# Output stores of a fused convolution and SiLU block: issued on Pool's queue instead of SyncE's

## The chip, the cores and the metric

The kernel runs on one core of a Trainium2 chip. The metric is the device time of one execution in microseconds, the median of several runs. Engines are named as in the profile: PE (TensorE), DVE (VectorE), ACT (ScalarE), POOL (GpSimd) and SP (SyncE, which computes nothing and here only issues DMAs).

## What is computed

Shapes: x is 8 x 4096 x 192, weight 8 x 7, w_in 192 x 2048, w_out 2048 x 192, all float32 as the kernel uses them.

```python
w = softmax(weight, axis=-1)                        # one 7-tap filter for each of 8 heads
x_pad = np.concatenate([zeros(B, 6, D), x], axis=1) # causal padding
out = np.einsum('hk,bskhg->bshg', w, windows(x_pad))
x = out.reshape(B * S, D)                           # 32768 x 192
h = x @ w_in                                        # "up" products
g = h * (1.0 / (1.0 + np.exp(-h)))                  # SiLU
return g @ w_out                                    # "down" products
```

## The kernel before, in words

The 32768 tokens are cut into 32 blocks of 1024, numbered 0 to 31. A block is two halves of 512 tokens, which lie in the two halves of the partitions. It goes through these stages:

- `load` (L181) brings x of a block into the tile `nat`, in three parts (tokens ld.0 to ld.2) of four DMAs.
- `turn_in` (L465, token i) transposes on DVE into `xt`. `halo_in` (token ha) fills the six columns ahead of it: Pool copies or clears the head of the first half (L486, L480), SP moves the second half's (L487). `tail_of` (L475) keeps the last columns for the next block.
- `conv` (token v) makes the seven taps: the first on ACT (L496), six on DVE (L499), back into `nat`.
- `spread` (L516, token sp) copies the result to both halves of the partitions, into `dup`, by DMA on SP. `win` (L533, L536, token w) makes sums and differences of it.
- `product` (L625, token P) and `plain` (L642, token L) are the up products on PE. The kernel uses a scheme with fewer products in place of ordinary ones; `sums_h` (L668, L674, L686) puts the pieces together on DVE and ACT and takes the SiLU into the tiles `g`.
- `sum_g` (L709, token t) subtracts pieces of `g` on DVE into tiles `t`: t.j0 and t.j1 go into one tile, t.j2 and t.j3 into another, for j from 0 to 3. `out_slot` (L741, token D) makes the down products on PE; D`i`.`je` stands for output piece i from chunk j, half e. `merge` (L804, L819) puts the output pieces together in `cmb`.
- `turn_out` (L829, token o) transposes `cmb` on DVE into the tile `osb`, in four parts o.0 to o.3. `store_out` (L838, token st) writes each part to `out_dram` with three DMAs of 64 KB, in rows of 128 bytes: 12 for a block.

`t` and `osb` share a pool of three buffers, and an osb is one buffer until all of its four parts are stored:

```python
tpool = ctx.enter_context(tc.tile_pool(name="tp", bufs=3))
    t[i // 2] = tpool.tile([P, 2, 2 * TB], F32, tag="t", name="t")
    osbs[b] = tpool.tile([P, 4, TB // SQ, SQ], F32, tag="t", name="osb")
```

The order of the work is written out by hand. `PLAN` is a string of tokens that is run once for each block; a token with "-" works on the block before, "=" on the one two before, "+" on the next. `pin` keeps the order of instructions on each engine and queue as the tokens give it; the head copy and clearing in `halo_in` on Pool are not pinned. In PLAN the tokens around the stores come in this order (others left out):

```
P5.0 ... | -D0.00 -t.01 | -D1.00 =o.2 | -D2.01 -t.03 | =st.2 | ... -t.02 | -D4.00 -t.10 | -t.11 | ... -t.12
... -t.13 | ... -o.1 | ... -st.1 | ... +ld.0 | ... sp.1 | ... +ha.0 | ... -st.0 | -st.3 ... t.00
```

So st.2 is the last of a block's stores, two turns after its up products, and t.10 of the next block comes soon after it. Semaphores are set by the framework from the tiles that instructions read and write.

The last block, 31, is stored by `finish` (L944) on SP's and ACT's queues. Blocks 0 and 1 are stored in a start-up order, `START`. In steady turns Pool runs one short instruction (L486 or L480).

Of the kernel before, what the change touches and what calls it, by code (L numbers as in the profile page):

```python
# [17 lines left out]
def kernel(  # L18
# [24 lines left out]
    nc = tc.nc  # L43
# [111 lines left out]
    def pin(ins):  # L155
        return tc.keep_in_program_order(ins)
# [677 lines left out]
    def store_out(b, i):  # L834
        for q in range((HD if b else P) // SQ):
            n, c = (i % 2, HD * (i // 2) + SQ * q) if b else (q // 2, R * i + SQ * (q % 2))
            pin(
                nc.sync.dma_start(  # L838
                    out=out_v[2 * b + n][:, :, c : c + SQ],
                    in_=osbs[b][SQ * q : SQ * q + SQ, i, :, :],  # L840
                )
            )
# [15 lines left out]
    def step(b, token):  # L858
# [19 lines left out]
        elif name[0] in "uXabS":  # L878
            sums_h(b, name, *digits)
        elif name == "t":  # L880
            sum_g(b, *digits)
        elif name[0] == "D":
            i, (j, e) = int(name[1]), digits
            for half in range(2) if i == 3 and b == NB - 1 else (None,):
                out_slot(b, j, i, e, half)
        elif name[0] in "Mzyx":
            merge(b, name, *digits)
        elif name == "o":
            turn_out(b, *digits)
        elif name == "st":  # L890
            store_out(b, *digits)
        elif name == "dp":
            next(downs)
        elif name == "cp":
            copy_plain(b, *digits)
        elif name == "go":
            pool.tensor_copy(warm, nats[1][:, digits[0], 0, 0:1])
            for g in (2, 3):
                for e in range(2):
                    combine(g, e)  # L900
        elif name == "ld":
            if b + 1 < NB:
                load(b + 1, digits)
        elif b + 1 < NB:
            {"i": turn_in, "ha": halo_in, "v": conv, "sp": spread, "w": win}[name](
                b + 1, *digits[: 1 + (name == "v")]
            )
# [203 lines left out]
```

## Time and profile before

| | |
|---|---|
| median of 3 runs | 2349.09 us (2348.8 to 2349.61) |
| the profiled execution | 2349.19 us, its span 2347.5 us |
| one turn of PLAN, from the timeline | 72.15 us |
| share of the span: PE, DVE, ACT, POOL | 100%, 89%, 51%, 4% |
| store `out_dram<-osb`, 64 KB, on SP | 376 issues, 2.0 us from issue to landing (median) |
| one store issue on SP (L838) | 0.50 us (median) |
| `dup<-nat`, 128 KB, on SP | 345 issues, 2.3 us to landing |
| `nat<-in_x_dram`, 64 KB, on SP | 382 issues, 2.4 us to landing |
| SP waiting at L838 for the transpose L829 | 1250.1 us in all, 66 times |

The span runs from the first to the last instruction; the execution's own time is 1.7 us longer. A row of the timeline has the start in us, the length in us, the engine (with "q" where only its queue works, as in issuing a DMA), the line, the operation, what it writes and reads, the shapes, how many instructions are merged in the row, and in brackets the idle time before it with what ended it. A row of a table by stretches has the stretch and its length, the busy us and instructions of PE, PEld (weight loads), DVE, ACT and POOL, then the granted clock of PE, the share of the DMA engines and GB/s. Matmuls overlap each other, so a row of one matmul is longer than the time from one start to the next.

### The profile page before, as it was taken

The numbers are of one execution on the slowest core, as the hardware profiler recorded it, in microseconds if no ns is written. First come the engines' busy times: TensorE is split into PE (matmuls) and PEld (weight loads), VectorE is DVE, ScalarE is ACT, GpSimd is POOL, SyncE is SP. The second block draws the span as 40 slices with busy tenths as digits, with TensorE's granted clock in tenths as the row PEclk, the third lists the DMA queues.
The fourth block names the chain that finished last, engine by engine and source line by source line (L and its number), as shares of the span: only waits on it lengthen the run. The fifth ranks groups of instructions, "written<-read, shape, count | busy, mean of one in ns | idle before, by whom it ended". The sixth has DMA issues, their size and how long they took to land.

```text
span 2347.5 us, 43988 instructions
## 1 busy us (share of the span) xinstructions
PE 2340.3 (100%) x17630; PEld 1061.0 (45%) x17630; DVE 2099.6 (89%) x2877; ACT 1187.3 (51%) x2275; POOL 96.8 (4%) x168
## 2 busy tenths in 40 slices
PE   9999999999999999999999999999999999999998
PEld 4344444444444444434444444444444444444445
DVE  8899989899899998998998999989999989899876
ACT  4345644456544466444564445654446644456443
POOL 4920000000000000000000000000000000000000
PEclk9999999999999999999999999999999999999999
DMA  7232212222121221222221222212222212222111
GB/s 158 52 66 48 47 27 47 38 53 53 29 41 36 53 53 31 39 43 46 53 49 31 42 38 53 53 29 42 36 53 53 38 33 45 43 53 44 20 24 25
DMA packets 451245, 106.56 MB, mean 45 GB/s; under 512 B 423584, under 2 KB 428704, under 8 KB 451040
## 3 DMA queue, kind: packets, MB, share of 16 engines
q1 hardware_dynamic: 447392, 101.78, 23.7%
q8 instruction: 138, 2.26, 0.4%
q0 software_dynamic: 448, 1.58, 0.3%
q10 hardware_dynamic: 3200, 0.39, 0.1%
q14 instruction: 67, 0.55, 0.1%
HBM read 31.46 MB, written 25.17 MB: 24 GB/s over the span
## 4 chain that ended last, share of the span: by engine, by line
PE 99%; DVE 0%; ACT 0%; issue 0%; ACTq 0%
PE ps L741 47%; PE ps L625 42%; PE ps L642 5%; PE ps L762 2%; PE ps L571 2%; PE ps L1010 1%; PE ps L423 0%; DVE t L709 0%; ACT g L686 0%; DVE cmb L163 0%; ACT u L163 0%; DVE osb L163 0%; DVE osb L829 0%; DVE g L668 0%; PE ps L449 0%
## 5 line engine op out<-in xcount | busy, mean ns | idle before, releaser
L625 PE MATMUL ps<-win,wr 64*128 64x512 f32 x1550 | 720.3, 597 | 0.0
L741 PE MATMUL ps<-g,wo 128*32 128x512 f32 x2976 | 702.4, 593 | 0.0
L625 PE MATMUL ps<-win,ws 64*128 64x512 f32 x1550 | 631.3, 595 | 0.0
L741 PE MATMUL ps<-t,wo 128*32 128x512 f32 (+2 forms) x4528 | 545.7, 446 | 0.0
L674 ACT COPY u<-ps 128x512 f32<-128x512 f32 x775 | 446.8, 586 | 173.6 <-PE ps L625 161.4
L741 PE MATMUL ps<-t,wx 128*32 128x512 f32 x2976 | 495.5, 592 | 0.1
L625 PE MATMUL ps<-dup,wr 64*128 64x512 f32 x868 | 425.4, 593 | 0.0
L499 DVE SCALAR_TENSOR_TENSOR nat<-xt,taps,nat 128x512 f32<-128x512 f32 x564 | 411.3, 753 | 3.8 <-ACT nat L496 3.6
L686 ACT ACTIVATE g<-g 128x512 f32<-128x512 f32 x465 | 286.1, 633 | 231.5 <-DVE g L668 231.5
L804 ACT COPY yx<-ps 32x512 f32<-32x512 f32 x150 | 86.9, 579 | 574.0 <-PE ps L741 572.3
L709 DVE TENSOR_TENSOR t<-g 128x1024 f32<-128x1024 f32 x248 | 300.6, 1219 | 51.1 <-PE ps L741 43.4
L625 PEld LDWEIGHTS ps<-win,wr 64*128 64x128 f32 x1550 | 275.6, 186 | 150.4 <-issue 67.8
L668 DVE TENSOR_TENSOR g<-u,ps 128x512 f32<-128x512 f32 x465 | 311.2, 680 | 28.8 <-PE ps L625 14.6
L625 PE MATMUL ps<-dup,ws 64*128 64x512 f32 x682 | 324.2, 599 | 0.0
L709 DVE TENSOR_TENSOR t<-g,t 128x1024 f32<-128x1024 f32 x248 | 301.8, 1217 | 12.2 <-PE ps L741 9.4
L741 PEld LDWEIGHTS ps<-t,wo 128*32 128x32 f32 x4528 | 186.7, 110 | 274.1 <-issue 247.6
L625 PEld LDWEIGHTS ps<-win,ws 64*128 64x128 f32 x1550 | 254.7, 186 | 110.5 <-issue 40.8
L686 ACT ACTIVATE g<-ps 128x512 f32<-128x512 f32 x465 | 266.8, 597 | 41.1 <-PE ps L625 38.4
L668 DVE TENSOR_TENSOR ps<-u,ps 128x512 f32<-128x512 f32 x310 | 214.7, 692 | 43.7 <-ACT g L686 19.0
L741 PE MATMUL ps<-g,wx 128*32 128x512 f32 x1488 | 250.5, 592 | 0.0
L741 PEld LDWEIGHTS ps<-g,wo 128*32 128x32 f32 x2976 | 170.2, 110 | 120.9 <-issue 118.9
L741 PEld LDWEIGHTS ps<-t,wx 128*32 128x32 f32 x2976 | 120.5, 110 | 217.5 <-issue 202.3
(90 smaller groups left out, 1764.5 us busy)
## 6 DMA issues: line engine op xcount, KB each, us to landing
dup<-nat SPq DMA_DIRECT2D x345, 128.0 KB, 2.3
nat<-in_x_dram SPq DMA_DIRECT2D x382, 64.0 KB, 2.4
out_dram<-osb SPq DMA_DIRECT2D x376, 64.0 KB, 2.0
raw<-in_moe_w_out_dram SPq DMA_DIRECT2D x8, 384.0 KB, 3.6
raw<-in_moe_w_in_dram SPq DMA_DIRECT2D x12, 192.0 KB, 4.7
ws<-wr POOLq DMA_DIRECT2D x8, 192.0 KB, 5.0
raw<-in_moe_w_in_dram SPq DMA_DIRECT2D x6, 128.0 KB, 3.1
xt<-xt SPq DMA_DIRECT2D x31, 4.5 KB, 1.9
```

Source lines behind the costliest of these rows:

```text
L499: nc.vector.scalar_tensor_tensor(out=dst, in0=src, scalar=tap, in1=dst, op0=ALU.mult, op1=ALU.add)
L571: nc.tensor.matmul(hs[a, n, e], rows(wr[j], e)[:, a, k, :], rows(d, e)[:, n, k, :], start=k == 0, stop=k == NK - 1,)
L625: nc.tensor.matmul(to[:, cols], raw(g, *LEFT[e][r], e), rhs[:, cols], start=first, stop=True, skip_group_check=True,)
L642: nc.tensor.matmul(banks[PLAIN_BANKS[n and 1 + e]][:, cols], rows(wr[j] if own == e else ws[j], e)[:, a, k, :], rows(dups[b], e)[:, SLOT[e ...
L668: pin(nc.vector.tensor_tensor(out_, u, v, op=op))
L674: pin(nc.scalar.copy(us[b, g, o][:, cols], t1[:, cols]))
L686: pin(nc.scalar.activation(h, src, AF.Silu))
L709: pin(nc.vector.tensor_tensor(t[i // 2][:, i % 2, :], u, v, op=ALU.subtract))
L741: nc.tensor.matmul(accs[b][at][SQ * q : SQ * q + SQ, to], lhs[:, e, SQ * k : SQ * k + SQ], rhs[:, e, ts(q, TB // 4) if i == 5 else to], st ...
L762: nc.tensor.matmul(banks[DOWN_BANKS[k]][R * n : R * n + R, :], wo[j][:, a, e, R * k : R * k + R], gs[b, j, a][:, n, e, :], start=j == 0 an ...
L804: pin(nc.scalar.copy(to, acc[3 * (name[0] == "x") + k][n:P, :]))
L1010: nc.tensor.matmul(by_pe[k][n], rows(diag, n)[:, k, i, :], rows(xts[0], n)[:, k, i : i + TB], start=i == 0, stop=i == K - 1,)
```

## The change

From block 2 on, `store_out` issues its DMAs from Pool (GpSimd) instead of SP. Where the stores stand in the order of tokens, what they move and the tiles are as before. `finish` is as before, too.

```diff
@@ -835,7 +835,7 @@
         for q in range((HD if b else P) // SQ):
             n, c = (i % 2, HD * (i // 2) + SQ * q) if b else (q // 2, R * i + SQ * (q % 2))
             pin(
-                nc.sync.dma_start(
+                (nc.gpsimd if b > 1 else nc.sync).dma_start(
                     out=out_v[2 * b + n][:, :, c : c + SQ],
                     in_=osbs[b][SQ * q : SQ * q + SQ, i, :, :],
                 )
```

## The prediction

> **What bounds the kernel now.** I read the page's first part, then the busy time of each engine in four block-long stretches, then the waits, then the timeline of one block.
>
> ```profile
> PE 2340.3 (100%) x17630; PEld 1061.0 (45%) x17630; DVE 2099.6 (89%) x2877; ACT 1187.3 (51%) x2275; POOL 96.8 (4%) x168
> ...
> PE 99%; DVE 0%; ACT 0%; issue 0%; ACTq 0%
> ```
> ```profile
> 1150.31:1222.45 72.14, 72.14 (x553) 32.69 (x552) 65.28 (x90) 37.15 (x72) 0.19 (x1) 1.00 0.24 43
> 1222.45:1294.60 72.15, 72.15 (x554) 32.72 (x553) 65.29 (x90) 37.16 (x72) 0.19 (x1) 1.00 0.24 43
> 1727.40:1799.55 72.15, 72.15 (x553) 32.66 (x552) 65.30 (x90) 37.15 (x72) 0.19 (x1) 1.00 0.24 43
> 1799.55:1871.70 72.15, 72.15 (x553) 32.80 (x552) 65.30 (x90) 37.17 (x72) 0.19 (x1) 1.00 0.24 43
> ```
>
> TensorE is busy all through, and every block takes 72.15 us. VectorE works 65.3 of those, Pool 0.2, so a change reaches the end only if it holds up PE. The queue view shows no PE wait that ends in a DMA. One transfer does hold up VectorE:
>
> ```profile
> DVE t L709 <- DMA out_dram<-osb: 5.7, 6, 1.3
> ```
>
> The subtraction L709 waits six times for a store (5.7 us in all, 1.3 at most). The timeline says which one. An ordinary block:
>
> ```profile
> 1223.77 0.70 DVE L829 STREAM_TRANSPOSE osb<-cmb 96x512 f32<-96x512 f32 x1
> ...
> 1224.49 1.41 SPq L838 DMA_DIRECT2D out_dram<-osb  x3
> 1226.00 4.33 SPq L516 DMA_DIRECT2D dup<-nat  x7
> ...
> 1227.89 1.21 DVE L709 TENSOR_TENSOR t<-g 128x1024 f32<-128x1024 f32 x1
> 1229.14 1.23 DVE L709 TENSOR_TENSOR t<-g,t 128x1024 f32<-128x1024 f32 x1
> 1230.28 1.22 DVE L709 TENSOR_TENSOR t<-g 128x1024 f32<-128x1024 f32 x1
> ```
>
> The last transpose of a block (token o.2) ends at 1224.47, its three stores (st.2) follow, and t.10 starts at 1227.89. The pool of `t` tiles has three buffers, two of them hold t.00 to t.03, and the third is the osb that these stores read: t.10 needs all three landed. Stores land 2.0 us after issue, so at about 1227.4: half a microsecond in hand.
>
> A block where SP was slow to issue the same three stores:
>
> ```profile
> 1801.63 2.89 SPq L838 DMA_DIRECT2D out_dram<-osb  x3
> ...
> 1806.41 1.23 DVE L709 TENSOR_TENSOR t<-g 128x1024 f32<-128x1024 f32 x1 [1.31 <-DMA out_dram<-osb]
> ...
> 1810.61 1.22 DVE L709 TENSOR_TENSOR t<-g,t 128x1024 f32<-128x1024 f32 x1
> ...
> 1812.07 1.15 PE L741 MATMUL ps<-t,wo 128*32 128x512 f32 x12
> ```
>
> The issues took 1.48 us more, t.10 started 1.31 us late, and the stretch from 1799.55 still took 72.15. So 1.31 us of lateness is free. But hardly more: t.13 (the row at 1810.61) ends at 1811.83, and the product that reads it, D3.11, starts at 1812.07 after a weight load of 0.13. About 0.1 us is left, so **PE's tolerance is about 1.4 us**.
>
> **What the Trainium skill says.** "DMA: Bandwidth & Descriptors", section "SWDGE vs HWDGE vs iDMA": a DMA from Pool has its descriptors computed by software on Pool's cores, one from SP by hardware. The same page, "Latency and other measured facts", gives the first byte as about 1 us against 0.6. The trace agrees in direction: the same kind of halo load (L198, 384 elements of 4 bytes) landed 3.0 and 3.1 us after issue from Pool, 2.6 from SP. The section "Issuing engines are not separate DMA queues" says that all issuers share the same 16 DMA engines, and a second issuer saves only issue time; nothing in this trace speaks against it. "SBUF — State Buffer", section "Who interferes with whom", has VectorE instructions with two SBUF inputs contend with Pool instructions that read SBUF. Here L499 takes 0.75 us in steady blocks and 0.94 (median) between 85 and 125 us, while Pool combines weights; whether Pool's descriptor writing does the same no row shows.
>
> **The change, part by part.** Stores of blocks 2 to 30 move: 29 blocks of 12, 348 issues.
>
> *Removed from SP.* 12 issues of 0.47 us, 5.6 us a block, and the waits for osb (1250.1 us over the run, 66 times). Behind them on SP stand nat loads, dup copies and the halo copy. They go earlier, but nobody waits for them now (VectorE waited 0.7 us once for a nat load; PE never for dup), so this is worth 0. One side effect: the seven dup copies behind st.2 can go when the last product on the old dup is done, about 1222.5 instead of 1226.0, and so share the DMA engines with st.2. DMA share is near 0.9 while they run.
>
> *Added to Pool.* 12 issues at 0.7 to 0.9 us (L198: 0.87 and 0.72) make some 10 us in a 72 us block. Pool has room. In its queue stands one other job, the head copy L486 (0.19 us, at 1199.22). The order of tokens puts it after st.1 (osb ready at 1196.4) and before st.0 (ready at 1208.2), and even after st.0 or st.3 it would be done by about 1214, where the halo transfer it goes with lands (issued by SP at 1212.61, 1.9 us). Worth 0; if that cover went, the scaled copy L496 at 1217.15 would still leave 3 us.
>
> *st.1, st.0, st.3.* Later landings by a microsecond or two are hidden: the tile is not given back before st.2, at least 11 us on.
>
> *st.2, the part that counts.* On SP the third store starts 0.91 us after the first and lands 2.0 later: 2.9 from release. On Pool, with L198's prices: the third starts 0.87 + 0.72 = 1.59 after release and lands 3.1 later: 4.7. Shift: 1.8. The slow-issue block turned a shift of 1.48 into a lateness of 1.31, so 0.17 comes off: 1.6. Added: 512 elements instead of 384 (a 64-element Pool DMA, L347, took 0.523; (0.717 - 0.523)/320 is 0.6 ns an element, 0.08 for each of two issues), 0.15; and the dup traffic, 0.15 by my estimate, for which no row stands. Lateness of t.10: **about 1.9 us**. Above the tolerance: 0.5 us. PE is full, so what it loses there it doesn't make good. The wait falls on t.10 of blocks 4 to 31, 28 of them: 28 x 0.5 = 14 us.
>
> Behind t.10 on VectorE stand t.11 to t.13, a conv tap, and t.20. These pass the lateness to D2.11 (t.11 ends at 1230.37, its weight load is at 1232.57: 2.2 us of slack) and D3.11 (1.4). After that it melts: t.20, t.23 and t.30 wait 0.43, 0.20 and 1.19 us for PE in an ordinary block.
>
> *Bounds.* Below: a Pool issue of 0.52 (second of an L347 pair) and a landing of 2.4 (SP's 2.0 plus the 0.4 by which L198 differed) give 1.04 + 2.4 = 3.4, lateness 0.4, loss 0. Above: L347 landed 4.4 to 6.7 us after issue (192 KB, beside the heavy loads of the start); 1.6 + 5.0 = 6.6 is a lateness of 3.5, a loss of 2.1 a block, 59 us. Contention that slows VectorE is inside this upper bound. No gain is excluded by PE alone: its loads also wait for VectorE and ScalarE in the up products, some tenths of a microsecond a block.
>
> **Sum.** The profiled execution took 2349.19 (span 2347.5 and 1.7 around it), 0.1 over the median 2349.09. 2349.2 + 14 = 2363.
>
> **The rivals.**
>
> *The stores land in time* (0.30): no change, so not slower. It is decided at t.10: if the third store lands within about 1.6 us of its present time (1.4 of lateness and 0.17), D3.11 finds t.13 ready, and the time is 2349. For it: 1.31 us was absorbed, and the lower bound gives 0.4. The buffer could also be given out otherwise, t.10 taking the one that D4.00 frees at about 1228.7; then it is late by 0.9 whatever the stores do. Against it: both L198 landings.
>
> *Pool's descriptor writing and VectorE get in each other's way* (0.15): at 1224.5 to 1228 VectorE runs t.03, a tap and t.02, all with two SBUF inputs. If each Pool issue waits for one (1.2 us), the third store starts 2.4 after release, not 1.6, and if VectorE loses as much, lateness is near 3.3: loss 1.9 x 28 = 53, time 2402. For it: L499 under Pool load. Against: L347's issues took 0.52 beside a busy VectorE.
>
> *SP's freed queue helps* (0.05): dups and loads in hand early. PE loses some tenths a block to late VectorE in the up products; regaining 0.3 in 28 blocks gives 2341. Against: those waits are for arithmetic, not transfers.
>
> *That the edit does nothing* is excluded unless the stores stayed on SP's queue; the issue rows would tell.
>
> **How the numbers follow.** Late store, small loss: 0.50, 2363. A measurement here can tell about 0.2%, 4.7 us, from no change; a loss of 0.17 us a block is that bound. Part of the likeliest case lies below it, roughly balanced by the in-time case lying just above. Slower 0.50 + 0.15 = 0.65; same 0.30; faster 0.05. Range 2347 to 2398: from no change to a lateness of 3.1 (28 x 1.7 = 48 us), leaving out most of the faster case and the top of the contention case.
>
> **What the changed profile would show.** Right: st.2's issues on Pool at 0.7 to 0.95 us; landing near 3; nearly every t.10 waiting 1.5 to 2.5 us for out_dram<-osb; a loads-wait of PE for t at D3.11; the down products (in the timeline 35.7 us from the first start, 1222.45, to the last) longer by half a microsecond, the up products as now. Wrong: t.10's wait under 1.4 and blocks of 72.15; or long Pool issues with L499 or L709 slower than 0.75 and 1.22; or a block that grows outside the down products, which would put the cause elsewhere.

## The result, and the profile after

The kernel with the stores on Pool's queue takes **2355.44 us** (median of 9 runs, 2354.01 to 2356.58) against 2349.09 (9 runs, 2348.8 to 2349.8): 1.0026 times the time before, 95% interval 1.0017 to 1.0035. That is slower by 6.35 us, on the side that was forecast, and less than half of the 14 us forecast. The profiled execution took 2355.44 us with a span of 2353.5, so 6.0 us more span than before.

The page of the profile after:

```profile
span 2353.5 us, 44146 instructions
...
PE 2346.0 (100%) x17630; PEld 1102.3 (47%) x17630; DVE 2100.2 (89%) x2877; ACT 1187.4 (50%) x2275; POOL 321.1 (14%) x516
...
q0 software_dynamic: 11584, 24.41, 6.4%
q8 instruction: 138, 2.26, 0.4%
...
PE 98%; DVE 1%; ACT 0%; DMA 0%; issue 0%; SPq 0%; POOL 0%; DVEq 0%; ACTq 0%
...
L838 POOL DMA_DIRECT2D out_dram<-osb x348 | 223.9, 649 | 1880.2 <-DVE osb L829 1873.3
...
L709 DVE TENSOR_TENSOR t<-g 128x1024 f32<-128x1024 f32 x248 | 302.1, 1218 | 59.1 <-DMA out_dram<-osb 37.9
```

The edit did what it says: 348 stores issue on Pool (516 instructions there instead of 168) and travel on a queue of their own, q0. VectorE's sum is as before (2100.2 against 2099.6). PE's busy time grew by 5.7 us with the same 17630 matmuls: matmuls overlap, so a PE that is held up still counts as busy nearly all the time, and the loss must be looked for elsewhere. The last two rows say where: L709 now has `out_dram<-osb` as the main thing that ends its waits. The list of waits, with total, times and longest:

```profile
DVE t L709 <- DMA out_dram<-osb: 37.9, 26, 3.2
```

Before it was 5.7 us in 6 times, 1.3 at most. So t.10 does meet the stores in nearly every turn, as forecast. The idle time of VectorE before t.10 is called its lateness here; the longest is 3.2 us. The loss is not even over the turns. Two turns in a row (stretch, length, then PE, PEld, DVE, ACT, POOL, clock, DMA share, GB/s); I call the first one turn 3 and count on from it:

```profile
357.00:429.14 72.14, 72.14 (x553) 32.74 (x553) 65.28 (x90) 37.15 (x72) 7.92 (x13) 1.00 0.23 43
429.14:502.92 73.78, 73.30 (x553) 37.68 (x552) 65.29 (x90) 37.13 (x72) 7.83 (x13) 1.00 0.23 42
```

The first takes what a turn took before, the second 1.64 us more. The timeline of turn 3, which lost nothing:

```profile
354.52 4.32 SPq L516 DMA_DIRECT2D dup<-nat  x7
...
358.31 0.70 DVE L829 STREAM_TRANSPOSE osb<-cmb 96x512 f32<-96x512 f32 x1
...
359.31 1.93 POOL L838 DMA_DIRECT2D out_dram<-osb  x3 [11.18 <-DVE osb L829]
359.33 4.49 SPq L181 DMA_DIRECT2D nat<-in_x_dram  x8
...
363.82 1.23 DVE L709 TENSOR_TENSOR t<-g 128x1024 f32<-128x1024 f32 x1 [1.31 <-DMA out_dram<-osb]
```

And of turn 4:

```profile
426.67 4.30 SPq L516 DMA_DIRECT2D dup<-nat  x7
...
431.44 5.68 SPq L181 DMA_DIRECT2D nat<-in_x_dram  x8
...
431.45 1.93 POOL L838 DMA_DIRECT2D out_dram<-osb  x3 [11.18 <-DVE osb L829]
...
437.81 1.22 DVE L709 TENSOR_TENSOR t<-g 128x1024 f32<-128x1024 f32 x1 [3.16 <-DMA out_dram<-osb]
...
440.35 0.12 PEld L741 LDWEIGHTS ps<-t,wx 128*32 128x32 f32 x3 [1.39 <-DVE t L709]
...
443.28 0.16 PEld L741 LDWEIGHTS ps<-t,wo 128*32 128x32 f32 x8 [0.84 <-DVE t L709]
```

Four things to see. Pool issues the three stores in 1.93 us in both turns (three of 0.65), as soon as the transpose is done, so Pool's queue is not what varies. t.10 is 1.31 us late in one turn and 3.16 in the other. And in the late turn PE's loads wait for t twice, with 1.39 and 0.84 in place of the usual 0.30: first at D2.11 for t.11, then at D3.11 for t.13. Less the usual 0.30 each that is 1.6 us, what the turn lost. The fourth thing is new beside the stores: the dup copies are now issued before the stores, and **eight loads of x** start within 20 ns of the stores in these two turns. On SP's queue before, four of those (ld.2) stood behind st.2 and the dup copies, four (ld.0) behind st.1, which waits for its transpose.

Per turn, the length of the down products (35.695 us where nothing is lost) follows the lateness of t.10:

| lateness of t.10, us | 1.31 | 1.37 | 1.48 | 1.52 | 1.59 | 1.66 | 1.92 | 2.08 | 2.41 | 2.65 | 3.16 |
|---|---|---|---|---|---|---|---|---|---|---|---|
| down products longer by, us | 0 | 0 | 0.003 | 0.039 | 0.110 | 0.177 | 0.433 | 0.596 | 0.923 | 1.163 | 1.668 |

That is max(0, lateness - 1.484), to 0.01 us, in all of them. Summed over the 28 turns from 2 to 29 it gives 6.35 us; the turns, from one start to the next, grew by 6.0 us in all, so about 0.3 us is made good outside the down products. Turns 4, 7, 10 and 13 give 4.93 of the 6.35, seven others the remaining 1.4, and the rest nothing. So two questions were left for experiments: is it really the meeting of t.10 with these three stores, and what makes the landing late in some turns only.

### The profile page after: what moved, and what is told of

It is laid out like the page before. It is cut to its first block, busy times and chain, and to the rows that moved or that the text cites. A ratio compares the mean times of both kernels' runs of the same rounds, so it can differ in the third digit from the quotient of the medians.

```text
span 2353.5 us, 44146 instructions
## 1 busy us (share of the span) xinstructions
PE 2346.0 (100%) x17630; PEld 1102.3 (47%) x17630; DVE 2100.2 (89%) x2877; ACT 1187.4 (50%) x2275; POOL 321.1 (14%) x516
## 3 DMA queue, kind: packets, MB, share of 16 engines
q1 hardware_dynamic: 263648, 78.95, 17.3%
## 4 chain that ended last, share of the span: by engine, by line
PE 98%; DVE 1%; ACT 0%; DMA 0%; issue 0%; SPq 0%; POOL 0%; DVEq 0%; ACTq 0%
PE ps L741 47%; PE ps L625 41%; PE ps L642 5%; PE ps L762 2%; PE ps L571 2%; PE ps L1010 1%; DVE t L709 0%; ACT g L686 0%; PE ps L423 0%; DMA out_dram<-osb 0%; DMA nat<-in_x_dram 0%; SPq L181 0%; DVE cmb L163 0%; DVE osb L829 0%; ACT u L163 0%
## 5 line engine op out<-in xcount | busy, mean ns | idle before, releaser
L741 PE MATMUL ps<-g,wo 128*32 128x512 f32 x2976 | 710.9, 593 | 0.0
L741 PE MATMUL ps<-t,wo 128*32 128x512 f32 (+2 forms) x4528 | 570.8, 446 | 0.0
L838 POOL DMA_DIRECT2D out_dram<-osb x348 | 223.9, 649 | 1880.2 <-DVE osb L829 1873.3
L499 DVE SCALAR_TENSOR_TENSOR nat<-xt,taps,nat 128x512 f32<-128x512 f32 x564 | 411.3, 753 | 3.8 <-ACT nat L496 3.6
L709 DVE TENSOR_TENSOR t<-g 128x1024 f32<-128x1024 f32 x248 | 302.1, 1218 | 59.1 <-DMA out_dram<-osb 37.9
L741 PEld LDWEIGHTS ps<-t,wo 128*32 128x32 f32 x4528 | 203.9, 110 | 268.6 <-issue 226.5
L709 DVE TENSOR_TENSOR t<-g,t 128x1024 f32<-128x1024 f32 x248 | 301.5, 1216 | 10.4 <-PE ps L741 4.9
L741 PEld LDWEIGHTS ps<-g,wo 128*32 128x32 f32 x2976 | 177.4, 110 | 125.2 <-issue 105.4
```

The costliest lines, as they stand in the source:

```text
L499: nc.vector.scalar_tensor_tensor(out=dst, in0=src, scalar=tap, in1=dst, op0=ALU.mult, op1=ALU.add)
L709: pin(nc.vector.tensor_tensor(t[i // 2][:, i % 2, :], u, v, op=ALU.subtract))
L741: nc.tensor.matmul(accs[b][at][SQ * q : SQ * q + SQ, to], lhs[:, e, SQ * k : SQ * k + SQ], rhs[:, e, ts(q, TB // 4) if i == 5 else to], st ...
L838: (nc.gpsimd if b > 1 else nc.sync).dma_start(out=out_v[2 * b + n][:, :, c : c + SQ], in_=osbs[b][SQ * q : SQ * q + SQ, i, :, :],)
```

## The experiments

Each is an edit of the changed kernel unless said otherwise; all are given against the kernel before, at 2349.04 to 2349.27 us on the chips concerned. Parts of the edits that only declare a tile or name a new token (`held_back`, `spare`, `hl`) are left out where they were shown or add nothing. R is the end of the transpose o.2, and times after R say when the last of the three stores of st.2 has landed. After the change that is about 4.5 us in the middle (3.9 to 6.3); on SP before it was 2.9.

### Which stores

**All but st.2 on Pool.**

```diff
-                (nc.gpsimd if b > 1 else nc.sync).dma_start(
+                (nc.gpsimd if b > 1 and i != 2 else nc.sync).dma_start(
```

> Only st.0, st.1 and st.3 go to Pool; st.2 stays on SP. Theory A (the loss is t.10 waiting for st.2 beyond the 1.48 us that PE tolerates, and nothing else): the time of before, 2349 us within 1, t.10 waiting as in before (6 times, at most 1.3 us). Rival C (Pool's descriptor writing or the moved queue costs something of its own, store by store): about three quarters of the loss of 6.3 us, near 2354.

Measured: 2348.74 us, 0.9998 (0.999 to 1.0006). What L709 waits for, in the list of waits:

```profile
DVE t L709 <- PE ps L741: 54.0, 78, 2.2
...
DVE t L709 <- DMA out_dram<-osb: 3.5, 5, 1.1
```

Most of it is for PE, whose products set buffers free (52.8 us before). For a store it waits five times, 1.1 us at most, under the 1.48 that is free; in the kernel before it was six times and 1.3. Nine of the twelve stores of a block cost nothing on Pool, and SP, freed of them, brings nothing either.

**Only st.2 on Pool** (`i == 2` in the same place).

> Only st.2 goes to Pool; the other nine stores of a block stay on SP. Theory A with traffic (the Pool path alone makes t.10 late by some 0.8 us, which is free; the x loads that SP now sends right behind the dup copies add the rest): st.1 on SP holds back four of the eight loads as before, so lateness lies between 0.8 and 1.5 and the time between 2349 and 2355, about 2351. Rival B (the Pool path alone makes the loss, traffic counts for nothing): 2355, as with all stores moved. Rival C: a quarter of the loss, 2351, but without t.10 waiting over 1.48 us.

Measured: 2357.14 us, 1.0034 (1.0021 to 1.0047). A miss, above the 2349 to 2355 expected: one part of four costs as much as all four (the intervals overlap). The turns show that it is not less. Beside st.2 run four loads of x, and the dup copies end later than with all four moved (in turn 3 the last of them land 1.0 to 2.3 us after R). The landing is at 4.2 to 4.8 us after R in an ordinary turn, and lateness averages 1.62 us (1.53 with all four moved). What the four loads and the late dup copies each add is not separated. Six turns have a landing of 5.4 to 6.5 us, 4, 7, 10 and 13 again among them; the worst has a lateness of 3.68. In three turns a Pool issue came half a microsecond late besides; why was not looked into.

### The meeting of t.10 and st.2

**The part o.2 gets a buffer of its own**, outside the pool that `t` uses. (Room for it came from laying two start-up constants into another tile.)

```diff
+        if b > 1 and i == 2:
+            lasts[b] = xpool.tile([P, TB // SQ, SQ], F32, tag="last", name="last")
...
-                    in_=osbs[b][SQ * q : SQ * q + SQ, i, :, :],
+                    in_=lasts[b][SQ * q : SQ * q + SQ]
+                    if b > 1 and i == 2
+                    else osbs[b][SQ * q : SQ * q + SQ, i, :, :],
```

> All stores on Pool as in the change, but the part that st.2 stores has a tile of its own (2 KB of a partition), so t.10 no longer takes a buffer that st.2 still reads. Theories A and B: t.10 never waits for a store, 2349 us within 1. Rival C: the wait is only a symptom and Pool's work or its transfers cost the time themselves: 2354 to 2356.

Measured: 2348.89 us, 0.9998 (0.999 to 1.0007). The timeline of turn 4 (line numbers are shifted by the edit):

```profile
430.74 1.93 POOL L847 DMA_DIRECT2D out_dram<-last  x3 [11.18 <-DVE last L828]
432.74 2.35 DVE L710 TENSOR_TENSOR t<-g 128x1024 f32<-128x1024 f32 x2
```

The stores are still on Pool, still take 1.93 us to issue and land as late as before (5.84 us after R in this turn). But t.10 is now the second of the two instructions in the last row, right behind t.02 with no gap, and the turn loses nothing.

**t.10 takes the other buffer.** The osb stays in the pool; only t.10 is written into the tile that D4.00 has just read.

```diff
-            t[i // 2] = tpool.tile([P, 2, 2 * TB], F32, tag="t", name="t")
+            if (j, i) == (1, 0) and b > 1:
+                t[0] = sums[b, 0][0]
+            else:
+                t[i // 2] = tpool.tile([P, 2, 2 * TB], F32, tag="t", name="t")
```

> The change, all stores on Pool, SP as free as after the change; only the tile of t.10 and t.11 is the one that t.00 and t.01 had (free when D4.00 has run), so that t.12 takes the buffer of the stored osb. Theory (the loss is the meeting of st.2's landing with t.10): t.10 starts 1.02 us late in every block, as in e8 to e10, which is under 1.48 and free; t.12 starts about 6.8 us after o.2, and st.2's third store, landing 4.3 to 6.3 as after the change, is always in time: 2349 us within 1. Rival (Pool path, traffic or fetches reach PE some other way): 2352 to 2356.

Measured: 2349.11 us, 0.9999 (0.9991 to 1.0007). In turn 4 t.10 waits about a microsecond for PE, in place of 3.16 for a store:

```profile
435.34 1.23 DVE L712 TENSOR_TENSOR t<-g 128x1024 f32<-128x1024 f32 x1 [1.04 <-PE ps L744]
```

A lateness of 1.04 is below 1.48 and costs nothing. These two kernels have all stores on Pool, the same traffic and the same issue times as the changed one, and run at the time of the kernel before. The whole loss is t.10 waiting for the landing of st.2. Nothing measurable is lost to Pool's work as such.

### Why the landing is late, and in some turns much later

**The loads held back.** ld.2, and with it what stands behind it on SP, goes behind a small DMA that reads t.13, so that the loads start only after st.2 has landed.

```diff
-        "-D1.30 v.22 | -D3.00 +ld.2 -t.13 | -D2.11 -a0.3 ...
+        "-D1.30 v.22 | -D3.00 -t.13 hl.1 +ld.2 | -D2.11 -a0.3 ...
+        elif name == "hl":
+            pin(nc.sync.dma_start(out=held_back, in_=sums[b - 1, 1][1][:, 1, 0:16]))
```

> All stores on Pool as in the change, but SP sends one small DMA that reads t.13's result ahead of the loads ld.2 and ld.0, so that these eight loads start some 9 us after o.2, as late as in the kernel before; the dup copies stay early. Theory A with traffic: st.2's third store lands about 3.9 us after o.2 instead of 4.3 to 6.3, t.10 waits about 0.8 us, time 2349 to 2350. Rival B: landings and time as after the change, 2355. If instruction fetches and not loads make the latest landings: landings of 3.9 in most blocks with a few over 5, about 2353.

Measured: 2351.16 us, 1.0009 (1.0 to 1.0017): two thirds of the loss are gone, between the 2349 to 2350 expected if loads are all and the 2353 expected if fetches are. Most turns now land at 3.7 to 4.0 us after R and have a lateness of 0.5 to 0.85. But turns 4, 7, 10 and 13 are late all the same. Turn 6, and turn 7, from the timeline:

```profile
579.83 1.22 DVE L709 TENSOR_TENSOR t<-g 128x1024 f32<-128x1024 f32 x1 [0.50 <-DMA out_dram<-osb]
```
```profile
653.77 1.23 DVE L709 TENSOR_TENSOR t<-g 128x1024 f32<-128x1024 f32 x1 [2.30 <-issue]
```

(The bracket of turn 7 names no store, but the store landed 5.53 us after R, 0.27 us before t.10 began.) No load, no dup copy runs at that time in either. What moved on the DMA engines between 3.3 and 4.9 us after R in turn 7 (queues, with packets, MB and the share of 16 engines):

```profile
q8 instruction: 1, 0.02, 3.4%
q0 software_dynamic: 2, 0.00, 1.8%
```

In the same stretch of turn 6 there is not a single packet. In turn 7 there is one packet of the queue that brings in instructions, 16 KB, which runs for 0.88 us on one of the 16 DMA engines. Fifteen of the third store's sixteen 4 KB packets had started by 3.02 us; the sixteenth started at 4.32, when the fetch ended (begun at 3.46, so 4.34 by the record), and the store landed 1.2 us after that. So the three stores were held up by one packet of 48. (The other record of q0 in the stretch is a small one that follows it.) In turns 4, 10 and 13, too, the sixteenth packet starts 0.01 us before the fetch's recorded end. The trace does not name the engine of a packet: that the two share one is inferred from this. In turn 7 the sixteenth packet was already some 0.4 us behind the others when the fetch's record begins, and why is not shown. Nor does every fetch near that time count: in turns 16 and 19 of this run one begins 3.42 and 3.52 us after R, all sixteen packets had started by 3.02, and the store landed in time.

The page counts 138 such fetches of 16 KB. With 35260 records of PE (17630 matmuls and as many weight loads) that is one for about 256 of them, and a turn has 1106, which makes 4.32 fetches. Their place therefore moves by a third of a fetch from turn to turn, and comes round nearly to the same place every third turn: hence 4, 7, 10, 13. That such a fetch belongs to PE is inferred from this count.

**The fetches shifted.** As the kernel just told, with 12 instead of 4 idle warm-up matmuls at the very start, which puts every later fetch at another place in the turns.

```diff
-    heat(4)
+    heat(12)
```

> The kernel with the loads held, with eight more idle matmuls at the start (heat(12) for heat(4)): 32 more records of PE before the blocks, so every later fetch of PE instructions (one for about 256 records) comes some 2 us earlier against the block. Theory of fetches (a 16 KB fetch that runs when the third store's packet is due holds up that packet on one DMA engine): the late landings of 5.3 to 5.5 us in the 4th, 7th, 10th and 13th block of the table vanish there, and others may come where fetches began 4.5 to 4.7 us after o.2 (22nd, 25th, 28th). If the late landings have to do with the position of those blocks (rings that wrap, start-up), they stay in the 4th, 7th, 10th and 13th. Time 2349 to 2352, plus what the idle matmuls cost at the start, at most 2 us.

Measured: 2354.34 us, 1.0023 (1.0014 to 1.0031). The warm-up cost 3.67 us at the start (the first down product begins at 63.70 us instead of 60.03), more than the 2 us allowed for it, so the total says little. The turns decide. Turn 7, which had the 2.30 just shown:

```profile
655.08 1.23 DVE L709 TENSOR_TENSOR t<-g 128x1024 f32<-128x1024 f32 x1 [0.66 <-DMA out_dram<-osb]
```

Turns 4, 7 and 10 lose nothing now, turn 13 0.1 us. In place of them turns 16, 19, 22 and 25 are late, by 1.79, 1.92, 2.19 and 2.04 us, with fetches that begin 2.68, 2.81, 2.95 and 3.00 us after R. Of the three turns named in advance 22 and 25 came true and 28 did not (its fetch begins at 3.75, and it lands at 3.67); 16 and 19 were not named. The stores, their queue and their traffic are the same in both kernels. The late turns moved with the fetches.

**The dup copies put back beside st.2**, behind a small SP DMA that reads the o.2 part of osb.

```diff
+        if b > 1 and i == 2:
+            pin(nc.sync.dma_start(out=held_back, in_=osbs[b][0:HD, i, 0, 0:16]))
```

> The change, with one small DMA on SP that reads the last part of osb ahead of the dup copies, so that SP waits for o.2 as in the kernel before: dup copies start at o.2 and run beside st.2 on Pool, the loads come after them, some 5 us after o.2. Theory with traffic, where any full traffic counts (the DMA engines are about 0.9 busy under dup copies): the third store lands 4.3 to 5 us after o.2, lateness 1.1 to 1.8, time 2351 to 2358. If only x loads (rows of 128 bytes from HBM) delay the stores: landing 3.7 to 3.9, time 2349 to 2351.

Measured: 2359.51 us, 1.0044 (1.0029 to 1.0058), a little over the 2351 to 2358 expected. The store lands at 4.7 us after R in the middle and at 5.6 to 6.5 in the five turns where a fetch begins between 3.4 and 4.4 us after R; lateness averages 1.78. The seven copies of 128 KB are now issued from 0.6 to 5.4 us after R, the loads come behind them, and the store lands later than beside eight loads of 64 KB. So the dup copies beside st.2 cost at least as much as the loads did: that they go ahead of it, on SP's emptied queue, spares the change that cost.

### Pool's queue, or any late landing

**Later still on Pool**: two Pool copies of 96 x 256 ahead of st.2's stores.

```diff
+        for _ in range(2 if b > 1 and i == 2 else 0):
+            pool.tensor_copy(spare, osbs[b][0:HD, i, 0:8, :].rearrange("p k c -> p (k c)"))
```

> The change, with two copies of a part of osb (96 x 256) on Pool ahead of st.2's three stores, so that these start later by x, some 0.7 to 1.2 us (its length is to be read from the trace). Theory A (PE loses just the part of t.10's lateness over 1.48 us): after the change the mean lateness is 1.53 us, so nearly every block now lies over the tolerance, and each of 28 blocks loses about 1.53 + x - 1.48: with x = 0.9 some 27 us, 2376; block by block the down products grow by lateness - 1.48. Rival (lateness is absorbed further on, and the 6 us come from elsewhere): under 2360.

Measured: 2370.41 us, 1.0091 (1.0074 to 1.0107). Slower, as expected, but not in the way expected. A copy took 1.76 us, three times what I had reckoned with and more, and the framework gave out the three buffers in another order (why is not shown): t.10 got the one that D4.00 frees (late by 1.02 us in every turn, at no cost), and t.12 the one of the osb. The row of the copies in the page, and the list of waits:

```profile
L163 POOL COPY spare<-osb 96x256 f32<-96x256 f32 x58 | 102.3, 1763 | 321.3 <-DVE osb L830 319.6
```
```profile
DVE t L709 <- DMA out_dram<-osb: 32.0, 28, 1.8
```

Those 28 waits are of t.12, 0.7 to 1.8 us on top of t.10's 1.02, and the down products grow by 0.3 to 1.4 us, about 22 us in all, near the growth of the span (2368.5 against 2347.5).

**st.2 on ACT's queue**, the other parts on Pool.

```diff
-                (nc.gpsimd if b > 1 else nc.sync).dma_start(
+                (nc.sync if b < 2 else nc.scalar if i == 2 else nc.gpsimd).dma_start(
```

> The change with st.2 alone issued on ACT's queue (hardware descriptors, as on SP) and the other nine on Pool: SP is as free as after the change, so dup copies and loads run as early. Theory (path and traffic add up: Pool's path lands the third store 0.8 us later than SP's, early loads add 0.6 to 0.9 and fetches more): third store lands 3.5 to 3.8 us after o.2, lateness 0.3 to 0.6, free but for fetches: 2349 to 2351, unless ACT, which now waits for o.2 in its own order, comes late itself. Rival (traffic alone makes the loss): landings and time as after the change, 2355.

**The kernel before, st.2 behind a small SP DMA** that waits for t.03.

```diff
-        "| -D2.01 -t.03 -S5.1 =st.2 | ...
+        "| -D2.01 -t.03 -S5.1 hl.1 =st.2 | ...
```

> The kernel before, no store on Pool; one small DMA on SP that reads t.03's result stands ahead of st.2, so the stores start some 1.5 us later: third lands about 4.5 us after o.2, lateness about 1.3 where no fetch falls in. Theory of the threshold (loss is lateness beyond 1.48, whatever makes it late): mostly free, 2349 to 2352. Rival (stores on Pool's queue cost by themselves): 2349 flat.

Measured: 2349.34 us, 1.0001 (0.9993 to 1.0009), with st.2 on ACT's queue, and 2349.15 us, 1.0001 (0.9992 to 1.0009), with st.2 later on SP. For the time both are inconclusive. In both, t.10 again got the buffer of D4.00 and was late by 1.02 us in every turn, whatever the stores did. They landed at 3.0 to 5.2 us after R from ACT's queue, mostly below 4.3, and mostly at 4.8 from SP in the other. What follows for the time is once more that a store which t.10 doesn't wait for may land at 4.8 for nothing. The landing from ACT's queue says more: 3.8 us after R in the middle, beside the same early loads, against 4.5 from Pool's queue and 2.9 from SP's without the loads. So traffic alone does not make the landing of 4.5; Pool's queue has a share, mostly because its third store starts 1.57 us after R and ACT's 0.99.

**The kernel before, st.2 behind a small SP DMA that waits for t.02**, some 3 us later.

```diff
-        "| -D2.01 -t.03 -S5.1 =st.2 | ... "-t.02 -S1.3 | ...
+        "| -D2.01 -t.03 -S5.1 | ... "-t.02 hl.0 =st.2 -S1.3 | ...
```

> As e9, but st.2 stands behind t.02 and a small DMA that reads its result: the stores start some 4 us after o.2, the third lands near 6.9, lateness 3.7. Theory of the threshold: each of 28 blocks loses 2.2 us, 62 us in all, 2411, with no store on Pool. If t.10 is given another buffer instead (the one that D4.00 frees, as happened in e5), the wait falls on t.12, later by 2.4 us, and the loss is less: 28 x 0.5 to 0.9, 2363 to 2374. Rival (the loss belongs to Pool's queue, not to when st.2 lands): 2349.

Measured: 2361.18 us, 1.0051 (1.0037 to 1.0064), just under the 2363 to 2374 expected for this order of buffers. Here no store is on Pool. One of the worst turns, with t.10 and then t.12:

```profile
801.07 1.23 DVE L709 TENSOR_TENSOR t<-g 128x1024 f32<-128x1024 f32 x1 [1.02 <-issue]
...
805.96 1.22 DVE L709 TENSOR_TENSOR t<-g 128x1024 f32<-128x1024 f32 x1 [2.40 <-DMA dup<-nat]
```

(By tile order it is the osb's buffer that t.12 waits for, and its last store landed 0.28 us before t.12 began; the dup copy named in the bracket came last by the record, as happens with waits for several semaphores.) The down products of this turn took 2.03 us more, which is 1.02 + 2.40 - 1.39; another turn with 1.02 + 1.46 grew by 1.09. So a late landing from SP is paid for in the same way, at nearly the same threshold: the loss goes by the time of landing and not by the queue.

No version was clearly faster than the kernel before. The two best, all but st.2 on Pool and the buffer of its own, lie within 0.02% of it.

## Why the prediction was right in kind and too large

By its own steps:

- **Issue on Pool.** Forecast: the third store starts 1.59 us after release, plus 0.15 for 512 elements. Measured: 1.57, every time. The first issue starts 0.29 us after R (0.03 on SP), and each takes 0.648. The price taken from L198 (0.87 and 0.72) was too high and the start-up of 0.29 was not in it; that the two errors cancel is luck. The 0.15 for more elements was wrong: an issue took 648 ns at 512 elements, less than L198 at 384.
- **Landing.** Forecast 3.1 us after issue, from L198. With no load beside it the third store landed 2.15 us after issue (3.72 - 1.57, loads held back), against 2.0 on SP. This term was 0.95 too large. The L198 rows stand among the heavy loads of the start (the DMA engines are 0.88 busy from 6 to 9 us) and probably carried that traffic with them; their landing beside idle engines was not measured.
- **Traffic beside st.2.** Forecast 0.15, for the dup copies. Measured 0.6 to 0.9 in an ordinary turn, and not from the dups, but from eight loads of x that the prediction had on its list of things that go earlier at a worth of 0. Their going earlier did bring PE nothing; that it would be at the same moment as st.2 was missed. The dup copies were forecast to start at about 1222.5, 2.0 us before R; they start 4.5 us before it, and the last of them lands about 1.6 us after it, as the third store is issued. "DMA: Bandwidth & Descriptors", section "Issuing engines are not separate DMA queues", is in the prediction with its statement that all issuers share the 16 DMA engines. The run with the loads held back agrees: 3.7 us instead of 4.5.
- **Lateness.** From the landing after R the prediction took 3.07 us (2.9 + 0.17) to get the lateness; measured 3.18 to 3.23, so 0.1 to 0.15 of lateness too much. Landing 0.95 too large, elements 0.15 too large, traffic 0.45 to 0.75 too small: with that, some 0.5 to 0.8 too large. Measured 1.34 us on average in the 24 turns without a late fetch and 1.53 over all 28, where 1.9 was forecast.
- **Tolerance of PE.** Forecast about 1.4, measured 1.48, at D3.11 as said. In the latest turns D2.11 is held up first: by 1.1 us (1.39 less the usual 0.30) for a lateness of 3.16, so its slack is 2.06, where 2.2 was read.
- **The step that failed: the size of the lateness, 1.9 us, and with it 0.5 us lost in each of 28 turns.** The mechanism was right, and the tolerance nearly so. The lateness was too large, mostly by the landing of 3.1 us where 2.15 was measured. An ordinary turn's 1.34 lies under the 1.48 that is free, and even the mean of all turns, 1.53, exceeds it by 0.05 only: 28 x 0.05 is 1.4 us, not 14.
- **A second step erred the other way: one lateness for all turns.** Measured lateness runs from 0.73 to 3.16. Most turns lie at or below 1.48 and lose nothing; four, where an instruction fetch meets the last store, lose 0.92 to 1.67. So the turns one by one give 6.35 us where their mean would give 1.4. The fetches, which make 4.93 of it, were not in the prediction. The spread only adds: with it around a mean of 1.9 the sum would have been 12.5 us (an estimate: each of the 28 latenesses raised by 0.37), so it is not what made the forecast too large. That the measured loss came as near to 14 as 6.35 is in part luck, from a missing spread against a lateness too large. The prediction's bounds for the lateness (0.4 to 3.5) were about the spread within one run, and were used only as bounds for a common value.

The rivals. *The stores land in time* is true turn by turn for over half of the turns, at the place and the price it gave (1.48 of lateness). *Pool's descriptor writing gets in VectorE's way* did not happen: L499 takes 753 ns and L709 1218 on average, as before to 1 ns (411.3 us for L499 in all, both times; 737 ns in the steady turns while st.2 is issued, 736 before), and the issues stay at 648 to 683 ns. "SBUF — State Buffer", section "Who interferes with whom", speaks of Pool instructions that read SBUF; here none of these rows moved. *SP's freed queue helps* found nothing to help: with only st.2 left on SP the time is that of before. The head copy L486 on Pool stayed ahead of its users, at a worth of 0 as forecast.

## What to carry to other kernels

When a wait has slack, a mean delay says little: list the delay turn by turn, subtract the slack from each, and add up what is left over. When transfers leave a queue, look at what stood behind them and will now start at the very moment the moved ones do. And before choosing an issuer for a store, look for who takes its buffer next; here another buffer for one tile made the issuer irrelevant.

## What the hardware showed that was not expected

- A DMA of 512 elements (64 KB in rows of 128 bytes) takes Pool 0.648 us to issue, with little spread (648 to 683 ns over 348), and starts 0.29 us after what releases it; SP issues the same in 0.50 (315 to 1983 ns) after 0.03.
- On Pool's queue each store of 64 KB goes out in 16 packets of 4 KB and as many of 4 bytes (96 records for three stores). Moving 348 stores took 183744 records from SP's queue (447392 to 263648), 528 for each: on SP a store goes out in 512 packets of 128 bytes and 16 of 4 bytes.
- A fetch of instructions (16 KB, 138 in a run) is one DMA packet of 0.9 to 1.7 us. In the four late turns of the run with the loads held back, the last packet of a store starts just as a fetch ends (within 0.02 us), and a landing of 3.7 us became 5.3 to 5.5. That both are on one engine is inferred.
- A Pool copy of 96 x 256 float32 beside VectorE's two-input subtractions took 1.76 us. Whether it is slowed by them was not tried.
